# A fused attention and GeGLU block: one gate/up tile moved from the attention stage to the paired stage, and GpSimd's sums and masks rearranged

## The chip, the core and the metric

The kernel runs on one core of a Trainium2 chip. The metric is device time in microseconds, the median of several runs. Engines are named as in the profile: PE (TensorE, matmuls; PEld are its weight loads), DVE (VectorE), ACT (ScalarE), POOL (GpSimd) and SP (SyncE, which issues most of the transfers).

## The reference

`x` is 2048 tokens by 640. It is normalised once, and two branches read the result; their sum is added to `x`.

```python
xn = layernorm(x)
q, k, v = split(xn @ wqkv)            # 32 heads of 20
p = softmax(q k^T * 20**-0.5)         # key j for query i only if 0 <= i - j < 256
A = (p v) @ wo
B = (gelu(xn @ w_gate) * (xn @ w_up)) @ w_down      # 1728 columns
out = x + A + B
```

## The kernel before

**Precision.** Every dense product is made of three: an operand is cut into a rounded high part and a remainder (ACT writes the high part, DVE or POOL the low one), and high x high, low x high and high x low are summed. So a dense tile of 128 x 512 over 640 rows is 15 matmuls (`dense_steps`, L107).

**Stages.** Tokens lie in four chunks of 512 (c = 0 to 3).
- *Start, to about 64 us:* layernorm, transposes into `xh` and `xl`, q/k tiles 0 and 5 of chunks 0 to 2, v tiles 0 to 7.
- *Ramp, to about 94 us:* twelve steps with negative slot numbers (-13 to -2) in `attention`. Each pulls eight filler matmuls, and every second one row maxima of the first units.
- *Attention, to about 546 us:* 32 units (eight groups of four heads by four chunks) of 14 slots each. A unit has row maxima (L492 matmuls, L502 on DVE) for a later unit, scores and exponentials (L557, L559), masks on POOL (`clear`, L572 and L575), the product with v (`av_unit`, L600) and its sum and store.
- *Paired stage, to about 805 us:* `gate_up_pair` makes a gate tile and an up tile for two chunks at once with sums of operands, 54 matmuls per pair of chunks instead of 60. It needs sums of the chunks of `x`; these are made earlier, in the attention stage, and kept in DRAM (`td`).
- *Last stage:* the products with `w_down` and `wo` (L1224).

**What sets the order.** In the attention stage the order on PE, ACT, DVE and POOL is written out by hand; `at` and `defer` put a function into a later slot. SP's order is made by the framework. An engine takes its instructions in its order, and each waits for what it needs.

**The filler.** Between the steps of attention PE takes dense matmuls from the generator `filler`: q/k tiles 0 and 5 of chunk 3, then the weights of tiles 1 and 6 are split (`split_qk`, POOL at L100), then v tiles 8 to 15 (through `v0`) and q/k tiles 1 to 4 and 6 to 9, the second half of v, and gate/up tiles 0 to `NFA - 1` and the last, half as wide one's weights. `RATE` is the number of filler matmuls per unit.

**From PE to DRAM (`save_qk`).** The bank `ps_d` (two buffers) of a q/k tile is cut into three bf16 parts: ACT writes the upper part into `pt` (two buffers, L277), DVE the remainder into `r` (one buffer, L273), ACT the middle part (L255), POOL the lowest, called *pt* below (L259). Then `pt` goes to DRAM, and `load_stack` (L467) fetches q and k for a unit from there.

**The sums (`x_sums`).** Per pair of chunks p, half of rows k and half of columns there are ten operations of POOL on 128 x 256 (s1 to s10, L738). They fill four tiles `tx` (numbers 1, 2, 4, 3 in order of time) in two buffers; each is stored to `td` by SP (L742). In all 80 operations and 32 stores. They stand in the first three slots of units 2 and following.

Of the kernel before, what the change touches and what calls it, by code (L numbers as in the profile page):

```python
# [13 lines left out]
OP = mybir.AluOpType  # L14
# [14 lines left out]
SR = 3 * DH  # L29
QROWS = 64 + SR  # L30
NS = 14
RATE = 30.9
LAST = 8
V1_SLOT = 169
MXD = 7
KSLOT = 9
LAG = 3, 5, 4, 4, 4, 4, 3, 3, 4, 3, 2, 1, 1, 1
NFA = 3
HD = D // 2
HR = 5  # L40
NQD = 9
OWN = 4, 5
WARM = 64
XS0, XSN = 2, 3
HELD = 10, 11, 12
RAMP = 4.0
GAP = 16
# [20 lines left out]
def block_kernel(ctx, tc, x, wqk, wv, wgu, wdo, wdl, out):  # L68
    nc = tc.nc
# [21 lines left out]
    td = [{i: dram.tile([128, 2, C], F32, name=f"td{p}{i}") for i in (1, 2, 3, 4)} for p in range(NC // 2)]  # L91
# [108 lines left out]
    def at(slot, fn, *a):  # L200
        acts.setdefault(slot, []).append((fn, a))
# [17 lines left out]
    def defer(n, fn, *a):  # L219
        if now[0] is None:  # L220
            fn(*a)
        else:
            at(now[0] + n, fn, *a)
# [93 lines left out]
    def proj_v(w, t, where=None):  # L317
        wh, wl, vt = w
        ts = slice(t * 128, (t + 1) * 128)
        pool, tag = where or (psd, "dn")  # L320
        ps = pool.tile([128, C], F32, name="ps_v", tag=tag)
        yield from dense_steps(ps[:, 0:320], lambda k: xh[:, k, ts], lambda k: xl[:, k, ts],
                               lambda k: wh[:, k, :], lambda k: wl[:, k, :], KT, 0.65)
        defer(1, save_v, ps, vt, t)
# [95 lines left out]
    v0 = []  # L420
    with tc.tile_pool(name="lp", bufs=1, side="right") as lp:
# [12 lines left out]
        v0 = v0[0]  # L434
# [89 lines left out]
    def pieces(c):  # L524
        b = 4 * c
        X = [(b, 0, 0, 384)] + ([(b - 2, 384, 0, 128)] if c else [])
        Y = [(b + 1, 0, 128, 384), (b + 3, 384, 384, 128)]
        Z = ([(b - 1, 0, 0, 256)] if c else []) + [(b + 2, 256, 256, 256)]
        return X, Z, Y

    def diag_tail(kb, col, q0, n, c):
        r = []
        for i in range(n // 128):
            dist = 4 * c + q0 // 128 + i - kb
            if dist == 0:
                r.append((col + 128 * i, True))
            elif dist == 2:
                r.append((col + 128 * i, False))
        return r
# [25 lines left out]
    def clear(u, bi, js):  # L565
        c = u % NC
        pt = pts[u, bi]
        for p in pieces(c)[bi]:
            for col, diag in diag_tail(*p, c):
                a, n = pt[:, js, col:col + 128], js.stop - js.start  # L570
                if diag:
                    nc.gpsimd.affine_select(out=a, in_=a, pattern=[[0, n], [1, 128]], compare_op=OP.is_ge,  # L572
                                            fill=0.0, base=0, channel_multiplier=-1)
                else:
                    nc.gpsimd.affine_select(out=a, in_=a, pattern=[[0, n], [-1, 128]], compare_op=OP.is_ge,  # L575
                                            fill=0.0, base=-1, channel_multiplier=1)

    def av_unit(u):
        g, c = divmod(u, NC)
# [110 lines left out]
    def filler():  # L690
        yield from proj_qk(0, w0, 3)
        yield from proj_qk(5, w5, 3)
        ws = [split_qk(raw) for raw in raws1]
        v1 = []
        prep = load_v(1, v1)
        pending = True
        for s, (kind, i) in enumerate(sets[:-1]):
            nxt = []
            after = sets[s + 1]
            for c in range(NC):  # L700
                if kind == "qk":
                    if i == 1 and c < 2:
                        for t in range(8 + 4 * c, 12 + 4 * c):
                            yield from proj_v(v0, t)
                    yield from proj_qk(i, ws[0], c)
                    if i == 2 or i == 3 and c == 0:
                        next(prep)
                    yield from proj_qk(i + 5, ws[1], c)
                    if i == 3 and c == 0:
                        next(prep)  # L710
                else:
                    yield from gate_up_fill(i, ws, c)
                if c == 0:
                    raws = [load_qk(after[1]), load_qk(after[1] + 5)] if after[0] == "qk" else load_gu(after[1])
                if c in (1, 2) and c <= len(raws):
                    nxt.append(split_later(*pools[(s + 1) % 2], raws[c - 1]))
                if pending and now[0] >= V1_SLOT:
                    pending = False
                    run(prep)
                    for j in range(4):  # L720
                        vtiles[4 + j] = v1[0][2][j]
                    for t in range(NB):
                        yield from proj_v(v1[0], t)
            ws = nxt
        rest.append(ws)

    def x_sums(p, k, half):
        w = C // 2
        a, b = (slice((2 * p + i) * C + half * w, (2 * p + i) * C + half * w + w) for i in (0, 1))
        eh, el = xh.bitcast(F32), xl.bitcast(F32)  # L730
        live = {}

        def tile_of(i):
            live[i] = ap.tile([128, w], F32, name="tx", tag="tx")
            return live[i]

        def pool(o, i, j, op):
            nc.gpsimd.tensor_tensor(out=o, in0=i, in1=j, op=op)  # L738

        def store(i):  # L740
            t = live[i]
            defer(2, lambda: nc.sync.dma_start(td[p][i][:, k, half * w:half * w + w], t))  # L742

        def s1():
            pool(tile_of(1), eh[:, k, b], eh[:, k, a], OP.subtract)

        def s2():
            pool(live[1], live[1], el[:, k, b], OP.add)

        def s3():  # L750
            pool(live[1], live[1], el[:, k, a], OP.subtract)
            store(1)

        def s4():
            pool(tile_of(2), eh[:, k + 2, b], live[1], OP.subtract)

        def s5():
            pool(live[2], live[2], el[:, k + 2, b], OP.add)
            store(2)

        def s6():
            pool(tile_of(4), eh[:, k + 2, a], live[2], OP.subtract)

        def s7():
            pool(live[4], live[4], el[:, k + 2, a], OP.add)
            store(4)

        def s8():
            pool(tile_of(3), eh[:, k + 2, b], eh[:, k, b], OP.subtract)

        def s9():
            pool(live[3], live[3], el[:, k + 2, b], OP.add)

        def s10():
            pool(live[3], live[3], el[:, k, b], OP.subtract)
            store(3)

        return s1, s2, s3, s4, s5, s6, s7, s8, s9, s10
# [24 lines left out]
    def attention():  # L803
        now[0] = -1
        load_stack(0)
        load_stack(1)
        load_stack(2)
        for i, (p, k, half) in enumerate((p, k, half) for p in range(NC // 2) for k in range(2) for half in range(2)):
            for j, fn in enumerate(x_sums(p, k, half)):
                m = 10 * i + j  # L810
                at(NS * (XS0 + m // XSN) + m % XSN, fn)
        for i in range(12):
            now[0] = i - 13
            for fn, a in tick():
                fn(*a)
            if i == 0:
                pull_max(1, now[0])
                pull_fill(RAMP)
                pull_max(1, now[0])
                debt[0] -= RAMP  # L820
            elif i % 2 == 0:
                pull_max(2, now[0])
            flush()
            pull_fill(2 * RAMP)
        pull_fill(GAP)
        for u in range(NU + 1):
            for i in range(NS):
                T = now[0] = NS * u + i
                for fn, a in tick():
                    fn(*a)  # L830
                if i in (0, 5, 9) or T == 3:
                    pull_max(2, T)
                if i == 0 and u:
                    if u == NU:
                        pull_fill(LAST)
                    av_unit(u - 1)
                    flush()
                    pull_max(2, T)
                if i % 2 and i < 12 and u < NU:
                    exp_piece(u, i - 1)  # L840
                    if i == 1 and u:
                        pull_fill(1)
                        debt[0] -= 1
                    exp_piece(u, i)
                flush()
                if u + 3 < NU and i in (KSLOT, 12):
                    load_stack(u + 3, (int(i == KSLOT),))
                pull_fill(RATE / NS)
        while acts:
            now[0] += 1  # L850
            for fn, a in tick():
                fn(*a)
            flush()
        now[0] = None
        run(fill)
        assert not acts
# [651 lines left out]
```

## Time and profile before

| what | us |
|---|---|
| median of three runs | 1047.88 (1046.38 to 1051.27) |
| the profiled execution | 1047.3 |
| its span | 1045.6 |
| attention's last product with v | ends at 546.3 |
| paired stage | 560.1 to 805.1 |

The profile is one execution. Its *span* runs from the first instruction to the last. *Busy* is the time in which an engine had an instruction at work. The *chain that ended last* is followed back from the end, at each step to what released it; what isn't in it can grow a little without making the kernel longer. In a row of a group stand line, engine, operation, output and inputs, the count, busy time and mean duration, and behind a second bar the engine's idle time before it and what ended that.

### The profile page before, as it was taken

To read this page: it belongs to the slowest core of one execution; us is meant where nothing else is said; L and a number is where in the kernel's file an instruction comes from. 1 tells how busy PE (TensorE), PEld (TensorE's weight loads), DVE (VectorE), ACT (ScalarE), POOL (GpSimd) and SP (SyncE) were. 2 spreads that over 40 slices of the span, in tenths; PEclk is the share of its full clock that TensorE was granted. 3 is DMA by queue.
4 is the path that set the end of the run, shared out by engine and by line. 5 is a ranking of instruction groups with operands and counts; after the bars stand their busy time and mean duration, and the time that the engine had idled before them with its cause. 6 is when DMAs were issued, how large, how long until landed. Compare 5 with 4: busy or idle time off the path is not lost.

```text
span 1045.6 us, 25699 instructions
## 1 busy us (share of the span) xinstructions
PE 1033.1 (99%) x9393; PEld 835.1 (80%) x9393; DVE 743.2 (71%) x2018; ACT 527.8 (50%) x1120; POOL 384.5 (37%) x622
## 2 busy tenths in 40 slices
PE   8999999999999999999999999999999999999998
PEld 7887666666787666666678888888888999999998
DVE  7845666677656576777736788775556888888887
ACT  4434666667666666666675232223234554433432
POOL 5122687979766787767470111101110000000000
PEclk9999999999999999999999999999999999999999
DMA  5642355564633364434125575763217874433333
GB/s 193 190 144 93 102 158 170 160 186 141 190 94 100 111 182 139 131 100 148 61 77 194 176 250 205 255 240 113 80 54 252 271 247 136 137 127 121 115 126 105
DMA packets 105192, 158.76 MB, mean 152 GB/s; under 512 B 15420, under 2 KB 60092, under 8 KB 105064
## 3 DMA queue, kind: packets, MB, share of 16 engines
q1 hardware_dynamic: 102680, 150.95, 44.9%
q10 hardware_dynamic: 2384, 6.16, 1.9%
q8 instruction: 74, 1.21, 0.5%
q14 instruction: 54, 0.44, 0.1%
HBM read 101.78 MB, written 54.92 MB: 150 GB/s over the span
## 4 chain that ended last, share of the span: by engine, by line
PE 94%; DVE 4%; ACT 1%; DMA 1%; issue 1%; SPq 0%; POOL 0%; DVEq 0%; ACTq 0%
PE ps_g L957 23%; PE ps L1224 23%; PE ps_d L107 20%; PE ps_e L557 8%; PE ps_v L107 6%; PE ps_o L600 5%; PE ps_m L492 5%; DVE junk L502 2%; PE ps_g L107 1%; DMA wr<-wqk 1%; PE ps_t L185 1%; PE ps_d L356 0%; DVE r L273 0%; DVE xl L194 0%; ACT P L559 0%
## 5 line engine op out<-in xcount | busy, mean ns | idle before, releaser
L502 DVE CUSTOM_DVE_ANT_0 junk<-ps_m,mask 128x320 bf16<-128x320 f32 (+2 forms) x512 | 242.7, 474 | 129.8 <-PE ps_m L492 71.9
L559 ACT ACTIVATE P<-ps_e 128x512 f32<-128x512 f32 (+2 forms) x384 | 198.7, 572 | 69.3 <-PE ps_e L557 68.8
L1224 PE MATMUL ps<-wb,at 128*128 128x320 f32 x999 | 155.9, 309 | 0.0
L1224 PEld LDWEIGHTS ps<-wb,at 128*128 128x128 f32 x999 | 148.9, 188 | 0.2
L572 POOL TENSOR_SCALAR_AFFINE_SELECT P<-P 128x256 f32<-128x256 f32 (+1 forms) x192 | 94.1, 492 | 73.4 <-ACT P L559 70.7
L557 PE MATMUL ps_e<-qs,ks 124*128 124x128 bf16 (+2 forms) x704 | 118.3, 278 | 0.1
L107 PE MATMUL ps_d<-xl,wqh 128*128 128x512 f32 x310 | 98.4, 421 | 0.0
L107 PE MATMUL ps_d<-xh,wqh 128*128 128x512 f32 x310 | 98.2, 421 | 0.0
L107 PE MATMUL ps_d<-xh,wql 128*128 128x512 f32 x310 | 97.6, 418 | 0.0
L100 POOL TENSOR_TENSOR wql<-wr,wqh 128x640 fp32r<-128x640 f32 x12 | 19.2, 1604 | 195.6 <-PE ps_g L957 151.0
L1224 PE MATMUL ps<-wt,at 128*128 128x320 f32 x552 | 88.9, 309 | 0.0
L557 PEld LDWEIGHTS <-ks 124*128 124x128 bf16 x704 | 49.5, 98 | 49.0 <-issue 34.3
L1224 PEld LDWEIGHTS ps<-wt,at 128*128 128x128 f32 x552 | 82.9, 188 | 0.1
L575 POOL TENSOR_SCALAR_AFFINE_SELECT P<-P 128x512 f32<-128x512 f32 (+1 forms) x144 | 76.4, 538 | 16.3 <-ACT P L559 14.6
L1178 ACT ACTIVATE at<-ss 128x512 fp32r<-128x512 f32 x59 | 37.3, 632 | 83.7 <-DVE ss L1062 83.6
L600 PE MATMUL ps_o<-P,v 64*32 64x320 f32 (+4 forms) x2816 | 74.2, 347 | 0.0
L259 POOL TENSOR_TENSOR pt<-r,pt 128x512 bf16<-128x512 f32 x40 | 46.5, 1164 | 67.2 <-ACT pt L255 61.0
L600 PEld LDWEIGHTS ps_o<-P,v 64*32 64x32 f32 x2816 | 50.9, 106 | 21.5 <-issue 0.9
L492 PE MATMUL ps_m<-ks,qs 60*64 60x320 bf16 (+3 forms) x1472 | 64.9, 260 | 3.1 <-DVE mx L502 1.5
L107 PEld LDWEIGHTS ps_d<-xh,wql 128*128 128x128 f32 x310 | 56.0, 189 | 10.1 <-issue 0.9
L492 PEld LDWEIGHTS <-qs 60*64 60x64 bf16 x1472 | 29.2, 105 | 43.6 <-issue 38.0
L107 PEld LDWEIGHTS ps_d<-xh,wqh 128*128 128x128 f32 x310 | 56.0, 189 | 9.7 <-issue 1.6
(195 smaller groups left out, 1968.4 us busy)
## 6 DMA issues: line engine op xcount, KB each, us to landing
hr<-hd SPq DMA_DIRECT2D x104, 128.0 KB
hd<-he SPq DMA_DIRECT2D x50, 256.0 KB
wr<-wgu SPq DMA_DIRECT2D x27, 320.0 KB
qs<-qd SPq DMA_DIRECT2D x64, 120.0 KB
ks<-kd SPq DMA_DIRECT2D x64, 120.0 KB
xi<-x SPq DMA_DIRECT2D x16, 320.0 KB
qs<-qd SPq DMA_DIRECT2D x64, 80.0 KB
ks<-kd SPq DMA_DIRECT2D x64, 80.0 KB
```

Of the source, the lines that this page charges most:

```text
L107: nc.tensor.matmul(ps, a(k), b(k), start=n == 0, stop=n == 3 * nk - 1)
L259: nc.gpsimd.tensor_tensor(out=pt[:, l, :], in0=r, in1=pt[:, 1, :], op=OP.subtract)
L492: nc.tensor.matmul(ps[64 * h:64 * h + 64, col:col + w], q[rows, j, q0:q0 + 64], ks_, start=True, stop=True, tile_position=(64 * r, 64 * h))
L502: nc.vector.tensor_tensor_reduce(out=junk[:, 0:n], in0=ps[:, 320 - n:320], in1=mask[:, 320 - n:320], scale=1.0, scalar=NEG, op0=OP.add, op ...
L557: nc.tensor.matmul(ps[:, col:col + n], k[0:QROWS, j, kc:kc + 128], q[0:QROWS, j, q0:q0 + n], start=True, stop=True)
L559: nc.scalar.activation(pt[:, j, lo:hi], ps[:, lo:hi], AF.Exp, scale=SCALE)
L572: nc.gpsimd.affine_select(out=a, in_=a, pattern=[[0, n], [1, 128]], compare_op=OP.is_ge, fill=0.0, base=0, channel_multiplier=-1)
L575: nc.gpsimd.affine_select(out=a, in_=a, pattern=[[0, n], [-1, 128]], compare_op=OP.is_ge, fill=0.0, base=-1, channel_multiplier=1)
L600: nc.tensor.matmul(os[r][32 * j:32 * j + 32, qa:qb], v[rows, w0_:w0_ + 32], pt[rows, j, col + qa - q0:col + qb - q0], start=r not in begun ...
L957: nc.tensor.matmul(ps, i, j, start=first and n == 0, stop=n == len(work) - 1, skip_group_check=True)
L1178: nc.scalar.activation(hi[:, 3:7], s, AF.Copy)
L1224: nc.tensor.matmul(ps[bank][:, 0:HD], *work[bank][j], start=bank not in begun, stop=final[p, bank] == n and j == len(work[bank]) - 1, skip ...
```

## The change

- `NFA` goes from 3 to 2 and `RATE` from 30.9 to 27.2: gate/up tile 2, the fourth that the filler would handle counting the half as wide one, is made in the paired stage.
- The sums of chunks 0 and 1 (p = 0, 40 operations) are placed in the ramp, three to a step, in slots -13 to 0; those of chunks 2 and 3 start in unit 12. Stores of p = 0 come one slot after their tile instead of two.
- In `clear` one instruction masks all blocks of a kind (on the diagonal, or two blocks from it) of a tile of exponentials; for that the blocks of `Y` change places, so that those of a kind lie side by side.
- v tiles 8 to 15 follow the q/k tiles 1 and 6 of chunks 1 and 2, where they stood ahead of those of chunks 0 and 1.

```diff
-RATE = 30.9
+RATE = 27.2
...
-NFA = 3
+NFA = 2
...
-XS0, XSN = 2, 3
+XS0, XSN = 12, 3
...
-        Y = [(b + 1, 0, 128, 384), (b + 3, 384, 384, 128)]
+        Y = [(b + 1, 128, 128, 384), (b + 3, 0, 384, 128)]
...
-        for p in pieces(c)[bi]:
-            for col, diag in diag_tail(*p, c):
-                a, n = pt[:, js, col:col + 128], js.stop - js.start
-                if diag:
-                    nc.gpsimd.affine_select(out=a, in_=a, pattern=[[0, n], [1, 128]], compare_op=OP.is_ge,
-                                            fill=0.0, base=0, channel_multiplier=-1)
-                else:
-                    nc.gpsimd.affine_select(out=a, in_=a, pattern=[[0, n], [-1, 128]], compare_op=OP.is_ge,
-                                            fill=0.0, base=-1, channel_multiplier=1)
+        cuts = sorted(x for p in pieces(c)[bi] for x in diag_tail(*p, c))
+        n = js.stop - js.start
+        for keep in (True, False):
+            cols_ = [col for col, diag in cuts if diag == keep]
+            if not cols_:
+                continue
+            m = len(cols_)
+            assert cols_[-1] == cols_[0] + 128 * (m - 1)
+            a = pt[:, js, cols_[0]:cols_[0] + 128 * m].rearrange("p j (b t) -> p j b t", b=m)
+            sign = 1 if keep else -1
+            nc.gpsimd.affine_select(out=a, in_=a, pattern=[[0, n], [0, m], [sign, 128]], compare_op=OP.is_ge,
+                                    fill=0.0, base=0 if keep else -1, channel_multiplier=-sign)
...
-                    if i == 1 and c < 2:
-                        for t in range(8 + 4 * c, 12 + 4 * c):
-                            yield from proj_v(v0, t)
                     yield from proj_qk(i, ws[0], c)
...
                     yield from proj_qk(i + 5, ws[1], c)
...
+                    if i == 1 and c in (1, 2):
+                        for t in range(4 + 4 * c, 8 + 4 * c):
+                            yield from proj_v(v0, t)
...
-            defer(2, lambda: nc.sync.dma_start(td[p][i][:, k, half * w:half * w + w], t))
+            defer(2 if p else 1, lambda: nc.sync.dma_start(td[p][i][:, k, half * w:half * w + w], t))
...
-                m = 10 * i + j
-                at(NS * (XS0 + m // XSN) + m % XSN, fn)
+                m = 10 * (i % 4) + j
+                at(NS * (XS0 + m // XSN) + m % XSN if p else m // XSN - 13, fn)
```

## The prediction, made before the changed kernel ran

> **What bounds the kernel now.** I read the page first, then the chain of work that ended last in order of time, then groups by shape, then single engines in the stretch that the change fills.
>
> ```profile
> span 1045.6 us, 25699 instructions
> PE 1033.1 (99%) x9393; PEld 835.1 (80%) x9393; DVE 743.2 (71%) x2018; ACT 527.8 (50%) x1120; POOL 384.5 (37%) x622
> ...
> PEclk9999999999999999999999999999999999999999
> ...
> PE 94%; DVE 4%; ACT 1%; DMA 1%; issue 1%; SPq 0%; POOL 0%; DVEq 0%; ACTq 0%
> ```
>
> TensorE carries 94% of the chain and GpSimd (POOL) 0%: work taken off GpSimd is worth nothing by itself, work taken off TensorE is worth its own time. The chain in order of time (start, length, what) shows how tight that is:
>
> ```profile
> 71.26 0.58 PE ps_v L107 x4
> 72.13 3.71 PE ps_v L107 x24
> 84.99 4.55 PE ps_d L107 x19
> 93.64 0.34 PE ps_e L557 x2
> ...
> 357.00 0.93 PE ps_d L107 x4
> 357.92 0.53 PE ps_e L557 x4
> 358.45 1.59 PE ps_d L107 x7
> ...
> 560.13 244.99 PE ps_g L957 x1080
> ```
>
> In the attention units (one per about 14.3 us) filler matmuls (L107) stand between scores with nothing idle. The paired stage is 1080 matmuls in 244.99 us, 0.227 us each, without a gap.
>
> **The change part by part.** *(1) Gate/up tile 2 leaves the filler.* That removes 4 chunks x 30 = 120 matmuls from the units. From the rows of 4 and 7, three more cost 0.66 us, 0.22 each; whole runs cost 0.23 each. So 26.4 to 27.6 us go; I take 27.0. In the paired stage the tile costs 54 matmuls per pair of chunks, 108 x 0.227 = 24.5 us. Net **-2.5 us**, bounds -1.9 and -3.1.
>
> It comes only if TensorE stays the bound in shorter units: RATE 27.2 for 30.9 takes 3.7 matmuls, 0.83 us, from each 14.3 us. Two units of before (length, then PE, PEld, DVE, ACT and POOL busy, clock, transfers), and the waits of VectorE for scores (us in total, times, longest):
>
> ```profile
> 191.13:205.47 14.34, 14.34 (x209) 9.58 (x215) 9.70 (x37) 10.31 (x21) 14.34 (x26) 1.00 0.56 161
> 360.34:374.67 14.33, 14.33 (x207) 9.48 (x213) 10.08 (x37) 10.32 (x21) 13.20 (x24) 1.00 0.61 176
> ```
> ```profile
> DVE junk L502 <- PE ps_m L492: 71.9, 82, 1.8
> ```
>
> VectorE and ScalarE need 10 of the remaining 13.5 us. VectorE waited for scores 82 times, 0.88 us on average, in some 4 x 31 = 124 groups of row maxima; those groups lose 0.21 us each and keep a margin. The other 42 may lose it: bounds 0 and 42 x 0.21 = 8.8 us. I take **+1.0**, near the margin's row.
>
> *(2) Masks and sums on GpSimd in the units.* It was full in the first of these units.
>
> ```profile
> L575 POOL TENSOR_SCALAR_AFFINE_SELECT P<-P 128x512 f32<-128x512 f32 x80 | 50.4, 644 | 16.3 <-ACT P L559 14.6 <-DMA ks<-kd 1.7
> L575 POOL TENSOR_SCALAR_AFFINE_SELECT P<-P 128x256 f32<-128x256 f32 x64 | 26.0, 407 | 0.0
> L738 POOL TENSOR_TENSOR tx<-tx,xl 128x256 f32<-128x256 f32 x48 | 36.4, 758 | 2.1
> ```
>
> Twice the elements cost 237 ns more, so an instruction has about 170 ns that don't depend on size. A unit's 11 masks become 8 (9 become 7 where c is 0): 24 x 3 + 8 x 2 = 88 fewer, 15 us. Units 2 to 11 lose three sums each, 2.2 us. So GpSimd falls to about 11.6 of 13.5 us in the first row and 12.7 in the second, which keeps its sums of chunks 2 and 3. All of this lies beside TensorE: 0 us. A mask with a fourth dimension isn't in the trace; should it cost twice as much as its 644 ns, TensorE's cover in the second row would be gone by about 1 us a unit, for some 13 units (in the upper bound below).
>
> *(3) Forty sums in the ramp.* The ramp runs from 64 us to the first score of unit 0 at 93.64. Here is its window (columns as above), GpSimd in it, then SyncE (it issues the transfers), then VectorE, then the sums and their stores (ns, shortest/median/longest):
>
> ```profile
> 64.20:93.60 29.40, 29.40 (x215) 24.30 (x215) 14.88 (x58) 10.11 (x32) 7.18 (x6) 1.00 0.47 142
> ```
> ```profile
> 62.42 1.17 POOL L259 TENSOR_TENSOR pt<-r,pt 128x512 bf16<-128x512 f32 x1 [2.28 <-ACT pt L255]
> 69.45 1.17 POOL L259 TENSOR_TENSOR pt<-r,pt 128x512 bf16<-128x512 f32 x1 [5.85 <-DMA qs<-qd]
> 70.57 3.10 POOL L100 TENSOR_TENSOR wql<-wr,wqh 128x640 fp32r<-128x640 f32 x2
> 74.05 1.17 POOL L259 TENSOR_TENSOR pt<-r,pt 128x512 bf16<-128x512 f32 x1 [0.37 <-ACT pt L255]
> ```
> ```profile
> 65.55 2.20 SPq L467 DMA_DIRECT2D ks<-kd  x6
> 67.79 2.20 SPq L467 DMA_DIRECT2D qs<-qd  x6
> 70.04 2.62 SPq L467 DMA_DIRECT2D ks<-kd  x6
> 72.77 0.82 SPq L268 DMA_DIRECT2D qd<-pt  x2
> 75.25 1.15 SPq L268 DMA_DIRECT2D kd<-pt  x2
> 76.44 0.91 SPq L234 DMA_DIRECT2D wr<-wqk  x2
> 78.25 1.06 SPq L467 DMA_DIRECT2D ks<-kd  x3
> ```
> ```profile
> 72.62 0.69 DVE L273 TENSOR_TENSOR r<-ps_d,pt 128x512 f32<-128x512 f32 x1 [1.58 <-ACT pt L277]
> ```
> ```profile
> L738 POOL TENSOR_TENSOR tx<-tx,xl x48: 722/733/1171, 122.8 to 491.2; 128x256 f32<-128x256 f32 x48
> L742 SPq DMA_DIRECT2D td<-tx x32: 337/346/570, 124.7 to 491.9; - x32
> ```
>
> GpSimd looks free there: 7.18 us of work in 29.4. But it takes its work in order, and in the built program of the changed kernel that order is (s1 to s10 a group's sums; "store 1" means: waits until tile tx 1 has been stored, since tx has two buffers):
>
> ```
> s1-s5 | store 1: s6 s7 | store 2: s8 s9 s10 | store 4: s1 s2
> pt(tile 0, chunk 3)  wql(tile 1)  wql(tile 6)  s3-s8  pt(5,3)  s9 s10 s1-s4  pt(1,0)
> s5-s10  pt(6,0)  s1-s6  pt(1,1)  s7-s10  pt(6,1)  first mask of unit 0
> ```
>
> The store of the first tx stands on SyncE behind the loads of units 0 to 2, which it issues without a pause until 72.7. From issue to landing I take 2.5 us: the load of ks at 78.25 reads what was stored at 75.25, so 240 KB landed in 3.0 us, and a tx has 128 KB. [...]
>
> Then: s1 to s5 from 63.6 to 67.3; s6 starts at 75.2. From there to the end of pt(1,1) GpSimd has 31 sums x 0.733 = 22.7, 5 pt x 1.165 = 5.8 and 2 wql x 1.55 = 3.1, so 31.6 us, and waits 4.3 us more for stores (0.3, 1.0, 0.3, 1.6, 1.1, as the steps fall out). Its stations: wql(1) ready at 83.4, pt(5,3) at 91.5, pt(1,0) at 97.4, pt(6,0) at 104.5, **pt(1,1) at 111.1**.
>
> Who waits: TensorE reaches tile 1's second five matmuls at 72.6, since v tiles 8 to 11, which covered the split, now stand behind; it waits for wql(1), 10.8 us. Then r, which has one buffer, lets VectorE write the next remainder only after the pt of the last; behind that instruction stand the row maxima, and the ps_d buffer (two) is free only after it. So v tile 10 needs the remainder of (6,1), which needs pt(1,1): 111.1 + 0.1 + 0.7 = 111.9. Without waits TensorE would be there at 71.26 + 60 q/k matmuls x 0.239 + 30 v matmuls x 0.155 + 4 groups of maxima x 0.4 = 91.9. The ramp grows by **20.0 us**. After it GpSimd has four sums and a pt left while the first exponentials run, so nothing more is lost; and the units, bound by TensorE, give nothing back.
>
> Bounds: landing in no more than the issue (0.35 us) gives pt(1,1) at 104.7, +13.6 us; 3.0 us gives +23; the slowest landing that a row shows, 5.5 us, gives +38:
>
> ```profile
> 552.32 0.50 SPq L880 DMA_DIRECT2D hd<-he  x1
> ...
> 557.82 0.69 DVE L879 TENSOR_TENSOR he<-ps_g,gs 64x512 f32<-64x512 f32 x1 [0.68 <-DMA hd<-he]
> ```
>
> That one fell into the busiest stretch of loads, so I stay at 2.5.
>
> *(4)* v tiles behind q/k alone are 0 us: the same matmuls, on TensorE in another order; what they stop covering is in (3).
>
> **Sum.** The profiled execution took 1047.3 us (span 1045.6), 0.6 under the median of 1047.88. 1047.3 - 2.5 + 1.0 + 20.0 = **1065.8 us**.
>
> **Rivals.** *A, faster:* the sums are hidden in the ramp, and GpSimd's relief speeds up VectorE. For it: VectorE's tiny negations take twice as long on average as the short ones, which can be GpSimd's doing:
>
> ```profile
> L512 DVE SCALAR_TENSOR_TENSOR nm<-mx,nm 128x16 bf16<-128x16 f32 x32 | 11.4, 355 | 1.1
> ```
> ```profile
> 78.82 0.17 DVE L512 SCALAR_TENSOR_TENSOR nm<-mx,nm 128x16 bf16<-128x16 f32 x1
> ```
>
> With 32 x 0.185 = 5.9 us back and nothing lost in the ramp: 1047.3 - 2.5 - 5.9 = 1038.9. It decides only if the ramp costs under 3 us, and GpSimd's own 31.6 us speak against that. *B, nothing:* TensorE isn't held, because wql or pt stand earlier than I read: 1045 to 1050. *C, the clock:* the ramp becomes stop and go. From 83.4 to 111.9 TensorE has 55 x 0.239 + 30 x 0.155 + 3 x 0.4 = 19 us of work; at half clock that is 38, 9.5 us more than the 28.5 there: 1075. The PEclk line shows nothing below 9, but also no wait so long. [...] *D, the units don't shrink with their filler:* +8.8 for +1.0 where VectorE binds, and up to 13 more with masks at twice the price: 1074 to 1086.
>
> **How the numbers follow.** Forecast 0.78 (own range 1058 to 1077), A 0.03, B 0.06, C 0.07, D 0.06. Range 1056 to 1080: the low end is the fastest landing with the best of the tile (1047.3 - 3.1 + 13.6 = 1057.8) and a little of B, the high end the landing of 3.0 with most of the bound on VectorE. Half a per cent, 5.2 us, is about what a measurement can tell from no change. Faster by more: 0.03; within: 0.06; slower: 0.91.
>
> **What would show it.** Sums on GpSimd from 64 us to past 110, TensorE waiting some 10 us for wql (L100), VectorE's remainders waiting for pt (L259), and unit 0's first score near 113 instead of 93.64. Units 13.5 us apart; attention's end near 540, the paired stage 269 us. I am wrong if the first score comes before 100, or if the units stay at 14.3.

## The result, and the profile after

| kernel | median us (range, runs) | ratio to before, 95% |
|---|---|---|
| before | 1047.13 (1046.26 to 1051.27, 4) | |
| after | 1073.37 (1073.08 to 1074.39, 4) | 1.0244 (1.0216 to 1.0273) |

The changed kernel is 26 us slower; 1065.8 was forecast, so 7.6 us are missing in the forecast's sum. The page of after (span; share of each engine; granted clock by slice; the chain that ended last, by engine):

```profile
span 1071.7 us, 25592 instructions
PE 1041.9 (97%) x9381; PEld 839.2 (78%) x9381; DVE 745.3 (70%) x2029; ACT 527.7 (49%) x1120; POOL 375.8 (35%) x526
...
PEclk9987999999999999999999999999999999999999
...
PE 86%; DVE 4%; ACT 4%; POOL 2%; issue 2%; DMA 1%; SPq 1%; ACTq 0%; DVEq 0%; POOLq 0%
```

TensorE's share of the chain fell from 94% to 86%. ScalarE's rose from 1% to 4%, GpSimd's from nothing to 2%, and issuing and SyncE's queue gained 1% each; VectorE's 4% and DMA's 1% are those of before. Two cuts place the time: the start of the first product with v (105.09 us before, 125.02 after) and that of the 32nd (543.78 and 545.34). Between them lie 31 units.

| stretch of the profiled execution | before | after | difference | forecast |
|---|---|---|---|---|
| to the first product with v | 105.1 | 125.0 | +19.9 | +20.0 |
| 31 units | 438.7 | 420.3 | -18.4 | -26.0 |
| the rest (paired and last stage) | 501.8 | 526.4 | +24.6 | +24.5 |
| span | 1045.6 | 1071.7 | +26.1 | +18.5 |

**The ramp.** GpSimd in order of time (the first and the third of its waits for stores, and the remainder pt that v tile 10 needs), then SyncE, then TensorE, then the stage's waits (us in total, times, longest):

```profile
75.72 0.72 POOL L741 TENSOR_TENSOR tx<-xh,tx 128x256 f32<-128x256 f32 x1 [8.50 <-DMA td<-tx]
...
101.44 0.72 POOL L741 TENSOR_TENSOR tx<-xh 128x256 f32<-128x256 f32 x1 [2.15 <-DMA td<-tx]
...
109.80 1.17 POOL L259 TENSOR_TENSOR pt<-r,pt 128x512 bf16<-128x512 f32 x1
```
```profile
72.16 0.82 SPq L745 DMA_DIRECT2D td<-tx  x2
```
```profile
83.66 2.50 PE L107 MATMUL ps_d<-xh,wql 128*128 128x512 f32 x5 [11.05 <-POOL wql L100]
...
113.49 0.50 PE L557 MATMUL ps_e<-qs,ks 124*128 124x384 bf16 x2
```
```profile
DVE r L273 <- POOL pt L259: 27.9, 5, 11.4
...
POOL tx L741 <- DMA td<-tx: 11.2, 4, 8.5
```

The first store is issued at 72.16, and the sum that waits for its tile starts at 75.72. wql is there at 83.66, pt(1,1) at 110.97, the first score at 113.49 instead of 93.49.

**The units.** TensorE between the two cuts, all of it and then the filler alone (us, times), before and after:

```profile
105.09:543.78 438.69, 436.13 (x5831) 297.71 (x5827) 288.71 (x1068) 294.90 (x643) 320.86 (x546) 1.00 0.44 132
```
```profile
105.09:543.78 438.69, 286.51 (x1045) 1.00 0.44 132
```
```profile
125.02:545.34 420.32, 414.12 (x5735) 279.68 (x5731) 275.59 (x1054) 287.40 (x640) 278.50 (x407) 1.00 0.43 127
```
```profile
125.02:545.34 420.32, 259.58 (x949) 1.00 0.43 127
```

The filler lost 286.51 - 259.58 = 26.9 us, as forecast (27.0). (It has 96 matmuls fewer and not 120, because of the new order of the v tiles: 60 narrow matmuls of v came in from the ramp, and 36 wide ones of q/k went out to it, which is about the same time.) The units lost only 438.7 - 420.3 = 18.4: 8.5 us are missing. TensorE's idle time grew from 438.69 - 436.13 = 2.6 to 420.32 - 414.12 = 6.2 us, 3.6 of them. A further part is in instructions that take longer, the 688 scores and the 1348 products for row maxima, as many as before:

```profile
105.09:543.78 438.69, 115.33 (x688) 1.00 0.44 132
...
105.09:543.78 438.69, 58.77 (x1348) 1.00 0.44 132
```
```profile
125.02:545.34 420.32, 117.64 (x688) 1.00 0.43 127
...
125.02:545.34 420.32, 59.81 (x1348) 1.00 0.43 127
```

That is 2.3 and 1.0 us; 1.6 are left that no group carries alone. Which units? A unit is counted here from one product with v to the next. Those with v tiles as filler shrank to 12.7 to 13.5 us. The third to the tenth and the twelfth, which have the first q/k tiles, stand at 13.7 to 14.5: together they gave back 1.6 us where 9 x 0.83 = 7.5 were forecast, so some 6 of the missing 8.5 us lie in these nine. Two units of after with the same work (169 and 170 matmuls), the first with q/k tiles, the second with a gate/up tile as filler:

```profile
178.94:193.41 14.47, 13.87 (x169) 8.82 (x165) 9.54 (x36) 10.06 (x20) 8.38 (x12) 1.00 0.48 143
...
451.83:465.36 13.53, 13.47 (x170) 8.61 (x166) 9.97 (x38) 9.40 (x20) 8.16 (x14) 1.00 0.39 119
```

0.94 us more for the same matmuls, with no engine beside TensorE over 10.1 of 14.47 us. VectorE and the chain at the end of that first unit:

```profile
193.53 0.69 DVE L273 TENSOR_TENSOR r<-ps_d,pt 128x512 f32<-128x512 f32 x1 [1.43 <-ACT pt L277]
194.13 0.48 DVE L502 CUSTOM_DVE_ANT_0 junk<-ps_m,mask 128x320 bf16<-128x320 f32 x1
...
196.06 0.49 DVE L502 CUSTOM_DVE_ANT_0 junk<-ps_m,mask 128x320 bf16<-128x320 f32 x1
```
```profile
191.99 0.59 ACT P L559
192.58 0.36 ACT wvh L301
192.94 0.49 ACT pt L277
...
196.06 0.49 DVE junk L502
...
196.61 0.33 PE ps_m L492 x3
```

It can be read as a hand-over: on ScalarE the upper part of a q/k tile (L277) stands behind exponentials and a split weight; VectorE's remainder waits 1.43 us for it, row maxima stand behind the remainder, and TensorE's next products wait for their banks.

### The profile page after: what moved, and what is told of

Same layout as the page of the kernel before. It is cut to its first block, busy times and chain, and to the rows that moved or that the text cites. A ratio compares the mean times of both kernels' runs of the same rounds, so it can differ in the third digit from the quotient of the medians.

```text
span 1071.7 us, 25592 instructions
## 1 busy us (share of the span) xinstructions
PE 1041.9 (97%) x9381; PEld 839.2 (78%) x9381; DVE 745.3 (70%) x2029; ACT 527.7 (49%) x1120; POOL 375.8 (35%) x526
## 4 chain that ended last, share of the span: by engine, by line
PE 86%; DVE 4%; ACT 4%; POOL 2%; issue 2%; DMA 1%; SPq 1%; ACTq 0%; DVEq 0%; POOLq 0%
PE ps_g L960 25%; PE ps L1227 22%; PE ps_d L107 13%; PE ps_e L557 7%; PE ps_v L107 6%; PE ps_o L603 5%; PE ps_m L492 4%; DVE junk L502 2%; ACT P L559 2%; PE ps_g L107 1%; POOL tx L741 1%; ACT pt L277 1%; PE ps_t L185 1%; DMA td<-tx 0%; SPq L467 0%
## 5 line engine op out<-in xcount | busy, mean ns | idle before, releaser
L578 POOL TENSOR_SCALAR_AFFINE_SELECT P<-P 128x512 f32<-128x512 f32 (+2 forms) x248 | 155.9, 652 | 92.4 <-ACT P L559 90.0
L557 PE MATMUL ps_e<-qs,ks 124*128 124x128 bf16 (+2 forms) x704 | 120.6, 278 | 1.5 <-ACT P L559 0.3
L107 PE MATMUL ps_d<-xh,wql 128*128 128x512 f32 x270 | 89.4, 433 | 11.1 <-POOL wql L100 11.1
L107 PE MATMUL ps_d<-xh,wqh 128*128 128x512 f32 x270 | 88.0, 426 | 0.4 <-DVE r L273 0.4
L107 PE MATMUL ps_d<-xl,wqh 128*128 128x512 f32 x270 | 86.6, 426 | 0.0
L492 PE MATMUL ps_m<-ks,qs 60*64 60x320 bf16 (+3 forms) x1472 | 67.1, 261 | 6.9 <-DVE mx L502 3.9
L989 ACT ACTIVATE hr<-hr 128x512 f32<-128x512 f32 x22 | 13.9, 632 | 111.2 <-DVE hr L963 111.2
L960 PE MATMUL ps_g<-xh,wqh 128*128 128x512 f32 x198 | 66.4, 389 | 0.0
L960 PE MATMUL ps_g<-xl,wqh 128*128 128x512 f32 x198 | 66.3, 389 | 0.0
L960 PE MATMUL ps_g<-xh,wql 128*128 128x512 f32 x198 | 66.3, 389 | 0.0
```

The source lines that it names most:

```text
L107: nc.tensor.matmul(ps, a(k), b(k), start=n == 0, stop=n == 3 * nk - 1)
L492: nc.tensor.matmul(ps[64 * h:64 * h + 64, col:col + w], q[rows, j, q0:q0 + 64], ks_, start=True, stop=True, tile_position=(64 * r, 64 * h))
L557: nc.tensor.matmul(ps[:, col:col + n], k[0:QROWS, j, kc:kc + 128], q[0:QROWS, j, q0:q0 + n], start=True, stop=True)
L578: nc.gpsimd.affine_select(out=a, in_=a, pattern=[[0, n], [0, m], [sign, 128]], compare_op=OP.is_ge, fill=0.0, base=0 if keep else -1, chan ...
L960: nc.tensor.matmul(ps, i, j, start=first and n == 0, stop=n == len(work) - 1, skip_group_check=True)
L989: nc.scalar.activation(g2, g2, AF.Gelu_apprx_tanh)
```

## The experiments

Two theories were to be told apart. **T1:** the ramp's 20 us are GpSimd's order, sums and waits for stores. **T2:** the units lack 8.5 us because ScalarE, idle under the product with v and full otherwise, bounds those with q/k tiles. Rivals of T2: GpSimd's load, and VectorE. The cuts of the table above, in the profiled execution of each kernel (us):

| kernel | median (ratio, 95%) | first score | to first product with v | 31 units | rest |
|---|---|---|---|---|---|
| sums in the units | 1055.37 (1.0074, 1.0052 to 1.0096) | 93.25 | 104.8 | 422.0 | 528.6 |
| ramp sums alone | 1067.27 (1.0193, 1.0171 to 1.0214) | 104.54 | 123.6 | 438.8 | 502.2 |
| no wait for stores | 1063.15 (1.0156, 1.0127 to 1.0184) | 105.33 | 116.9 | 420.3 | 528.0 |
| rate alone | 1059.05 (1.0110, 1.009 to 1.013) | 93.01 | 104.5 | 424.2 | 529.2 |
| masks and v order alone | 1046.44 (0.9994, 0.9985 to 1.0003) | 92.39 | 104.0 | 437.8 | 502.8 |
| middle part on GpSimd | 1073.44 (1.0240, 1.0219 to 1.0261) | 111.76 | 123.3 | 421.4 | 528.6 |
| middle part twice | 1076.84 (1.0268, 1.0247 to 1.0290) | 113.44 | 125.0 | 423.6 | 526.1 |
| remainder later | 1074.93 (1.0251, 1.0231 to 1.0270) | 114.87 | 126.4 | 420.5 | 526.2 |
| remainder later, weights on GpSimd | 1070.80 (1.0220, 1.0206 to 1.0234) | 111.71 | 123.2 | 417.9 | 528.0 |
| sums from unit 9 | 1061.62 (1.0140, 1.0112 to 1.0167) | 91.89 | 103.4 | 426.8 | 526.7 |
| sums from unit 9, middle part on GpSimd | 1065.13 (1.0165, 1.0144 to 1.0187) | 91.58 | 103.1 | 432.0 | 527.6 |
| masks, v order, remainder later | 1046.93 (0.9995, 0.9986 to 1.0005) | 94.36 | 106.0 | 437.7 | 503.4 |

The runs were taken in three sets, each with its own runs of the kernel before (medians 1047.0 to 1048.3), to which the ratios refer. The profiled execution is one of the timed ones and not always near the median: for "sums from unit 9" it is 3 us under it, for "no wait for stores" 4 us over it, the slowest of the four. Small differences of medians are therefore read by the stretches. The rest isn't the same to the microsecond either: the last stage, which no version changes, took from 240.5 to 243.6 us, and the first score of kernels without sums in the ramp came between 91.58 and 94.36.

**The ramp. 1: the changed kernel with its sums back in the units.**

```diff
-XS0, XSN = 12, 3
+XS0, XSN = 2, 3
...
-            defer(2 if p else 1, lambda: nc.sync.dma_start(td[p][i][:, k, half * w:half * w + w], t))
+            defer(2, lambda: nc.sync.dma_start(td[p][i][:, k, half * w:half * w + w], t))
...
-                m = 10 * (i % 4) + j
-                at(NS * (XS0 + m // XSN) + m % XSN if p else m // XSN - 13, fn)
+                m = 10 * i + j
+                at(NS * (XS0 + m // XSN) + m % XSN, fn)
```

> The changed kernel with the sums where they were before (three a unit from unit 2), the rest as changed. Theory: the ramp's growth of 20.0 us (first score of unit 0 at 113.49 us instead of 93.49) comes from the 40 sums in GpSimd's queue alone. Then the first score is back near 93.5 us and the time is 1073.4 - 20.0 = 1053.4 us, or up to 2 more, since GpSimd has 2.2 us more work in units 2 to 11. The remaining 6 us above the kernel before are those of the shorter units. Rival: the v tiles moved behind q/k cause part of the ramp's wait by themselves (they covered the split of tile 1's weights): the first score then stays above 97 us and the time above 1057 us.

1055.37, at the edge of T1's range. The first score is back at 93.25: the sums' place is worth 18 of the 26 us, and v tiles behind q/k tiles are not what delays the ramp. The units take 1.7 us more than in the changed kernel, and the eleventh alone accounts for it (15.3 us for 13.4), by a stall of VectorE that the last section shows.

**2: the kernel before with the ramp sums alone** (the same three edits the other way round).

```diff
-XS0, XSN = 2, 3
+XS0, XSN = 12, 3
...
-            defer(2, lambda: nc.sync.dma_start(td[p][i][:, k, half * w:half * w + w], t))
+            defer(2 if p else 1, lambda: nc.sync.dma_start(td[p][i][:, k, half * w:half * w + w], t))
...
-                m = 10 * i + j
-                at(NS * (XS0 + m // XSN) + m % XSN, fn)
+                m = 10 * (i % 4) + j
+                at(NS * (XS0 + m // XSN) + m % XSN if p else m // XSN - 13, fn)
```

> The kernel before with one part of the change: sums of chunks 0 and 1 in the ramp, the others from unit 12. Theory (GpSimd's queue holds r, whatever the order of v): pt(5,3) comes near 91 us and the remainder of (6,0) only near 110 us, so the first score is near 113 us and the time 1047.1 + 20 = 1067 us. Rival: the moved v tiles expose the wait; with the old order TensorE loses only the wait of v tile 9 for the remainder of (5,3), about 9 us: first score near 103 us, 1056 us.

The time is T1's, the place is partly not. The first score comes at 104.54, 11 us late instead of 20, and the other 7 are lost behind it, where v tiles stood ahead of the late tiles and TensorE reaches the wait later:

```profile
109.79 0.41 PE L107 MATMUL ps_v<-wvh,xh 128*128 128x320 f32 x1 [3.86 <-DVE r L273]
```

The first product with v is 18.5 us later than before, so the order of the v tiles moves the loss more than it changes it. Not all of the 7 us are that wait, though: it is 3.9 us long, and behind it TensorE had half its clock for 6.8 us (granted 0.50 from 110.9 to 117.8). That the sum comes to T1's figure is in part luck.

**3: the changed kernel without waits for stores:** the ramp's sums get a place of their own each, in two tiles of exponentials that are idle then.

```diff
-            live[i] = ap.tile([128, w], F32, name="tx", tag="tx")
+            if p:
+                live[i] = ap.tile([128, w], F32, name="tx", tag="tx")
+                return live[i]
+            if not spare:
+                t = ap.tile([128, 4, C], F32, name="P", tag="P", bufs=3)
+                spare.extend(t[:, j, h * w:h * w + w] for j in range(4) for h in range(2))
+            live[i] = spare.pop(0)
```

> The changed kernel, but the sums of the ramp go to two of the three tiles that the exponentials use later, so no sum waits until an earlier one is stored. Theory: GpSimd then works without a pause from 63.2 us: 36 sums x 0.785, 5 pt and 2 splits are 36.9 us, pt(1,1) is ready at 100 us instead of 110.97, the first score comes near 102.5 us and the time is 1062.5 us. So about 11 of the 20 us are waits for stores (the first, 8.5 us, because the store stands on SyncE behind the loads of units 0 to 2), and 9 are GpSimd's own work. Rival: stores don't matter, something else holds TensorE (SyncE's later loads, ScalarE): 1073 us.

1063.15 for 1062.5. GpSimd now works without a pause until pt(1,1), here the last of its rows; the rows of TensorE are the ten matmuls ahead of the v tiles:

```profile
69.81 0.74 POOL L749 TENSOR_TENSOR P<-xh 128x256 f32<-128x256 f32 x1
70.63 1.56 POOL L749 TENSOR_TENSOR P<-P,xl 128x256 f32<-128x256 f32 x2
...
99.80 1.17 POOL L259 TENSOR_TENSOR pt<-r,pt 128x512 bf16<-128x512 f32 x1
```
```profile
94.36 2.33 PE L107 MATMUL ps_d<-xh,wql 128*128 128x512 f32 x5
96.49 2.01 PE L107 MATMUL ps_d<-xl,wqh 128*128 128x512 f32 x5
```

pt(1,1) is ready at 100.97 instead of 110.97, much as expected. The first product with v comes only 8 us earlier, at 116.9 instead of 125.0: TensorE's ten matmuls take 4.0 us, at half the clock (granted 0.50 from 94.6 to 98.0), where ten such took 2.3 at 82.1 in the same run. In the medians the gain is 10 us. So of the ramp's 20 us, 8 to 10 are waits for stores and most of the rest is GpSimd's own work in the queue. T1 is shown; the sizes of its parts are known to some 2 us.

**The rate and the masks. 4: the kernel before with gate/up tile 2 out of the filler alone.**

```diff
-RATE = 30.9
+RATE = 27.2
...
-NFA = 3
+NFA = 2
```

> The kernel before with one part of the change: gate/up tile 2 in the paired stage, 27.2 filler matmuls a unit. Theory: the units lose to ScalarE what they lost in the changed kernel (7.5 us of 26), whatever GpSimd does: 1047.1 - 27.0 + 24.5 + 8.5 = 1053 us. Rival 1: GpSimd, with the old masks and three sums a unit from unit 2, is what holds units 2 to 11 at 14.3 us: up to 8.5 us more, 1058 to 1062 us. Rival 2: with the old order of v the units shrink in full: 1045 us.

1059.05: 6 us over the theory's figure, in the range of the rival that names GpSimd. The stretches don't bear that rival out: of the 6 us, 4 are in the units, 2 of them the stall in the eleventh (15.5 us), and 3 are in the rest, by the varying last stage. Against experiment 1, which is this kernel with the new masks and the v order, the units take 424.2 instead of 422.0 us; the medians differ by 3.7. So with the lower rate those two parts bring something together, about 2 us in the units; 1.0 of it is the second unit, which has v tiles in experiment 1 and q/k tiles here. Masks and v order were not run apart at this rate. **5: they alone, at the old rate** (the diff of the change without `RATE`, `NFA` and the sums).

```diff
-        Y = [(b + 1, 0, 128, 384), (b + 3, 384, 384, 128)]
+        Y = [(b + 1, 128, 128, 384), (b + 3, 0, 384, 128)]
...
+            a = pt[:, js, cols_[0]:cols_[0] + 128 * m].rearrange("p j (b t) -> p j b t", b=m)
...
+                    if i == 1 and c in (1, 2):
```

> The kernel before with two of the four parts alone: two blocks of a kind masked at once, and v tiles behind q/k tiles; rate, gate/up tile and sums as before. Theory and prediction: GpSimd's saved 15 us lie beside TensorE, 0 us, 1046 to 1048. Rival (the relief of GpSimd counts in the units, as the 3.7 us between the two versions with the lower rate and the sums of before suggest): 1043 to 1045.

0.9994 with an interval that holds 1: nothing, as forecast. What GpSimd saves is worth nothing at the rate of before.

**The units. 6 and 7: one ScalarE copy taken away, and the same copy doubled.** The copy is the middle part (L255, 0.63 us), in the units of the changed kernel.

```diff
-            nc.scalar.activation(pt[:, 1, :], r, AF.Copy)
+            if now[0] is not None and now[0] >= 0:
+                nc.gpsimd.tensor_copy(pt[:, 1, :], r)
+            else:
+                nc.scalar.activation(pt[:, 1, :], r, AF.Copy)
```

> The changed kernel, except that in the attention units the copy of the middle part of a q/k tile (L255, 0.63 us on ScalarE, 29 times in units) is done by GpSimd. Theory (ScalarE, which has no work under the product with v and is full in the rest of a unit with q/k tiles, keeps those units at 13.6 to 14.4 us): ramp unchanged, first score at 113.5; units 2 to 9, 11 and 20 to 23 fall toward 13.4, 3 to 7 us in all, so 1066 to 1070 for 1073.4. Rival (VectorE or GpSimd keeps them there): no gain or some us more, 1073 to 1077, since GpSimd gets about 1.2 us per tile on top.

```diff
             nc.scalar.activation(pt[:, 1, :], r, AF.Copy)
+            if now[0] is not None and now[0] >= 0:
+                nc.scalar.activation(pt[:, 1, :], r, AF.Copy)
```

> The changed kernel with that copy done twice by ScalarE in the units: 29 more ScalarE instructions of 0.63 us, 18.3 us in all, nothing else touched. Theory (ScalarE bounds the units with q/k tiles): those units grow by most of what is added, so +10 to +18 us, 1083 to 1091. Rival (another engine bounds them and ScalarE has a margin of 3 us per unit, as its busy time of 10 in 13.6 us suggests): 1073 to 1076.

The 31 units of both (the fourth engine is ScalarE):

```profile
123.30:544.72 421.42, 414.81 (x5736) 279.99 (x5732) 277.64 (x1054) 273.02 (x612) 294.42 (x436) 1.00 0.43 127
```
```profile
124.97:548.56 423.59, 416.57 (x5736) 280.54 (x5732) 276.00 (x1054) 304.06 (x668) 278.49 (x408) 1.00 0.43 126
```

14.4 us less on ScalarE bring nothing (420.3 to 421.4), 16.7 us more cost 3.3. Experiment 6 alone would not settle it, for the copies went to GpSimd, which has 15.9 us more to do (294.42 for 278.50), and its "nothing" is a balance: the twelfth unit lost 0.8 us, while the thirteenth grew by 0.7 and the twenty-third by 0.9. Experiment 7 puts nothing on GpSimd, and 1076.84 lies far under the theory's range and just above the rival's. So T2 in this form falls: ScalarE's load as a whole does not set the units, though it has no 3 us of margin in each either. The copy L255 stands behind the remainder, outside the hand-over shown above.

**8: the hand-over itself.** In the changed kernel the remainder of a q/k tile goes behind the row maxima at a unit's end, by one slot in slots 10 to 13.

```diff
-            late(middle)
+            if now[0] is not None and now[0] >= NS and now[0] % NS in (10, 11, 12, 13):
+                defer(1, late, middle)
+            else:
+                late(middle)
```

> The changed kernel, except that in the units VectorE's remainder r of a q/k tile (L273) whose slot is one of the last four of a unit is put one slot later, behind the row maxima that it stood ahead of. Theory (not ScalarE's load but the hand-over keeps the units long: at the end of a unit the upper part of a q/k tile stands on ScalarE behind the last exponentials, VectorE's remainder waits up to 1.8 us for it, eight row maxima stand behind the remainder, and TensorE waits for their banks): the units at whose end such a remainder stands lose 0.5 to 1 us each, some six of them, so 1068 to 1071 for 1073.4. Rival (TensorE waits for something else there): 1073 to 1074.

**9: the same, and ScalarE without the split weights** that stand among its exponentials.

```diff
-            nc.scalar.activation(hi, raw, AF.Copy)
+            nc.gpsimd.tensor_copy(hi, raw)
```

> As the last, and the high parts of the split weights in the units (ten copies of 128 x 640, 0.74 us each on ScalarE, among the exponentials) are made by GpSimd. Theory (what counts on ScalarE is only what stands between the scores and the next upper part or exponential that TensorE waits for): five of the ten stand in units with q/k tiles and bring up to 0.7 us each, 1 to 3 us more, 1066 to 1069. Rival (GpSimd's copy is later than ScalarE's and its queue passes it on): no gain or 1 to 2 us lost.

The unit that begins behind the chain shown above (193.41 to 207.54 in after, 14.13 us), in experiment 8 and in 9:

```profile
194.97:208.41 13.44, 13.38 (x192) 8.71 (x188) 9.74 (x36) 9.57 (x20) 9.29 (x15) 1.00 0.60 165
```
```profile
191.59:204.83 13.24, 13.24 (x192) 8.71 (x189) 9.74 (x36) 8.91 (x19) 9.82 (x15) 1.00 0.58 165
```

In this unit the hand-over cost 0.7 us, and it is gone. Over all units experiment 8 gains nothing (420.5): one unit lost 0.7, the one ahead of it grew by 0.2, and another by 0.9, where work of GpSimd and a weight's load of 5.3 us stand in the chain. Experiment 9 gains 2.4 us on after (417.9), nearly all of it in units with split weights and the unit behind one. Both fall short of what the theory in its second form expected by half or more. The 4 us between their medians come mostly from elsewhere: the ramp, the same program in both, had its first score at 114.87 in one and 111.71 in the other.

**Better versions. 10 to 12.** All eighty sums in units, four in each from unit 9 on; the same with the middle part on GpSimd; and masks, v order and the later remainder at the old rate.

```diff
-XS0, XSN = 12, 3
+XS0, XSN = 9, 4
...
-                m = 10 * (i % 4) + j
-                at(NS * (XS0 + m // XSN) + m % XSN if p else m // XSN - 13, fn)
+                m = 10 * i + j
+                at(NS * (XS0 + m // XSN) + m % XSN, fn)
```

> The changed kernel without the sums in the ramp: all eighty in the units, four to a unit from unit 9 on, stores two slots behind. Theory (ramp +20 us through GpSimd's order, and GpSimd's load in the units is not what keeps them long): first score near 93.3, 1053 to 1056, like the version with the sums from unit 2 on. Rival (GpSimd's load is what keeps units 2 to 9 long): those units fall to 13.4 us and the time to 1049 to 1052.

```diff
+            if now[0] is not None and now[0] >= 0:
+                nc.gpsimd.tensor_copy(pt[:, 1, :], r)
```

> Sums from unit 9 on and the middle part on GpSimd in the units, for ScalarE's sake. Theory: the gains add up, 1048 to 1052, by a little not under the kernel before (1047), since 24 us of the tile's matmuls are still paid in the paired stage and the units cannot give back more than 26. Rival (ScalarE is not what units wait for): 1053 to 1056.

```diff
-            late(middle)
+            if now[0] is not None and now[0] >= NS and now[0] % NS in (10, 11, 12, 13):
+                defer(1, late, middle)
+            else:
+                late(middle)
```

> The last one (masks and v order alone) with the remainder put one slot later as in the first of this batch. Theory: in units of 14.3 us the hand-over is mostly covered by the filler, 0 to -2 us, 1045 to 1047.5. Rival: the same gain as in the first, 1043 to 1044.

1061.62, 1065.13 and 1046.93. The first two miss by 6 and 13 us. Two units carry most of it, 16.1 and 18.3 us long in experiment 10, 15.5 and 20.5 in 11. In the longer one GpSimd is busy for 15.6 and 18.0 us and stands in the chain with masks, split weights and pt, so it is the bound there. The rows ahead of it show where its backlog comes from: in the unit before, a sum had waited 4.6 and 4.1 us for the store of an earlier one (td<-tx), as in the ramp, with everything else of GpSimd behind it; and TensorE, kept waiting, then had half its clock for 3.4 and 6.8 us. Units 2 to 8 have no sums here, but they have none in the changed kernel either, so their length (13.7 to 14.4) says nothing on the rival that blames GpSimd for the early units. Experiment 1 does: there the third to the tenth unit have three sums more each, 2.2 us of GpSimd, and take 112.2 us in all, against 112.5 in the changed kernel. GpSimd's load does not set them. The third is the kernel before, within its interval: no version here beats it.

## Why the prediction was right and wrong

*The ramp (+20.0, measured +19.9 to +20.0).* Right, by its stations: wql 83.4 and 83.66, pt(1,1) 111.1 and 110.97, first score 113 and 113.49; experiment 3 shows the store's part, experiment 1 the whole. The landing of 2.5 us, an estimate from the 3.0 us of a row with 240 KB, was short: 3.56 from issue to the next sum. The waits behind it were shorter in return, 2.7 us in three instead of 4.3 in five. The last link, v tile 10 held by pt(1,1), is less sure than its number: TensorE came to that tile at 111.75 straight from the tile before, and the remainder behind pt(1,1) had ended at 111.69. That the total is right to a tenth is partly luck: five executions of this same ramp had the first score between 111.71 and 114.87.

*The tile (-27.0 in the filler, +24.5 in the paired stage).* Right: 26.9, and

```profile
561.61 269.30 PE ps_g L960 x1188
```

against 244.99, so +24.3.

*Masks, v order (0).* Right at the old rate (experiment 5). At the lower rate the two together are worth about 2 us (experiment 1 against 4), which the forecast's 0 left out. How much of it is GpSimd's relief and how much the v order is not shown.

*The units, the step that failed.* "VectorE and ScalarE need 10 of the remaining 13.5 us", those groups "keep a margin", hence "+1.0". The term was 8.5 instead of 1.0, at its own upper bound of 8.8, and VectorE, the engine of that bound, was not the right one alone. Busy time says nothing of the margin of an instruction in a hand-over: an upper part behind exponentials, a remainder behind that, row maxima behind that. While a unit had 14.3 us of matmuls, the filler covered such waits; with 3.7 fewer it no longer does in most units with the first q/k tiles, while units with v tiles, which bring no such chain, shrank about as forecast. The chain shows this for one unit, and experiment 8 took it away there; for the others it is argued. The rows show TensorE's idle time growing by 3.6 us and its scores and row-maxima products stretching by 3.3.

Which hand-overs make up the 8.5 us is settled in part only. 2.4 go with the weights' high parts off ScalarE and the later remainder; ScalarE's load as a whole is ruled out by experiment 7, GpSimd's in the third to the tenth unit by experiment 1. Some 6 us stay open. The forecast's own sign, "units 13.5 us apart", could not have told: they are 420.3 / 31 = 13.56 apart after, but were 438.7 / 31 = 14.15 apart before, and not 14.3. A third bank for the row maxima or the scores, which might take TensorE's waits away one by one, was not tried.

*The rivals.* D (the units don't shrink with their filler) came about, on top of the forecast and not instead of it, without its dearer masks. C (the clock) came about as a fact (granted 0.50 for 5.0 and 3.4 us, not throughout) and cost nothing in the changed kernel: see below. A and B are out by experiments 2 and 5. The range's upper end of 1080 lies 3 us above what its own words add up to (1047.3 - 2.5 + 8.8 + 23 = 1076.6).

## What to carry to other kernels

Idle time of an in-order engine is room only for work that nothing urgent stands behind: forty sums, 29 us of work, cost 20 in a stretch in which the engine idled for 22, because the splits that TensorE needs queue behind them, and because two buffers tie the queue to a store that other loads delay (issued behind them at 72.16, the first held a sum for 8.5 us). When the bound engine's filler is thinned, price each hand-over between the other engines and not their busy shares. And check the price of a part at the operating point where it will run: masks and v order, worth 0 together under a full filler, were worth some 2 us under a thinner one.

## What the runs showed of the hardware

*The clock.* After its wait of 11 us TensorE worked for 5.0 us at half its clock (granted 0.50), and a second time for 3.4 us after the next waits, the last of 1.77 us. The rows are two of the first stretch and one of the second, then the same matmuls as in the second, in experiment 7 (columns as in the units' windows; the third value from the end is the granted clock):

```profile
83.66:88.10 4.44, 4.44 (x11) 3.47 (x12) 0.83 (x4) 0.00 (x0) 4.00 (x5) 0.50 0.26 84
88.10:95.00 6.90, 6.47 (x46) 4.51 (x45) 3.28 (x11) 1.82 (x3) 6.50 (x9) 0.96 0.68 209
...
102.16:106.37 4.21, 4.21 (x14) 3.17 (x13) 1.29 (x4) 0.63 (x1) 3.98 (x6) 0.59 0.26 79
```
```profile
101.36:105.63 4.27, 2.85 (x14) 1.91 (x13) 0.75 (x2) 0.02 (x1) 4.02 (x6) 1.00 0.27 84
```

Five matmuls took 2.50 us there, 1.32 at the full clock. Both stretches lay beside GpSimd's queue, which decides the ramp, and moved no station: in experiment 7, whose ramp is the same, the clock was full in the second stretch, TensorE waited for GpSimd instead, and the first score came at 113.44 for 113.49. It did cost time where TensorE's own work came last, as in experiments 2 (6.8 us at half the clock) and 3 (ten matmuls in 4.0 us for 2.3). The kernel before has such a stretch too, near its start (0.66 from 14 to 19 us, 0.50 from 15 to 17), shorter than a slice of its PEclk line, which shows 9 there. In the first stretch above the granted clock had fallen from 1.00 to 0.50 at about 75.0, within the wait that began at 72.6, and it was back at 1.00 by 88.7. What sets it is not shown: no run varies the length of a wait by itself.

*A tiny VectorE instruction that took over 20 times its usual time.* The negation nm<-mx on 128 x 16 takes 0.17 us as a rule (median 175 or 176 ns in before, after and experiments 1, 4 and 10). In those three experiments one of them took 3.5 to 4.3 us, in the same unit. VectorE and GpSimd in experiment 10:

```profile
247.38 4.30 DVE L511 TENSOR_SCALAR nm<-mx 128x16 bf16<-128x16 f32 x1
```
```profile
248.28 1.26 POOL L613 TENSOR_TENSOR ob<-ob,P 128x512 f32<-128x512 f32 x1
249.50 0.45 POOL L644 TENSOR_TENSOR wql<-wr,wqh 128x128 fp32r<-128x128 f32 x1
249.92 1.72 POOL L578 TENSOR_SCALAR_AFFINE_SELECT P<-P 128x512 f32<-128x512 f32 x2
```

GpSimd worked without a gap, and the negation ended at 251.68, when GpSimd's run did (251.64). In experiment 1 it is 252.21 and 252.18, in experiment 4 254.57 and 254.54. The two ends lie within 0.04 us of each other in each of the three runs, behind five or more of GpSimd's instructions in a row; no run varies this, so what held the negation is not shown. In experiments 1 and 10 it is the longest piece of the chain in its unit, which takes 15.3 and 16.1 us where the changed kernel takes 13.4.
